# Top-32 selection on rows folded to 304 elements, and both heads transposed in blocks

## The chip, the cores and the metric

The kernel runs on one core of a Trainium2 chip. The metric is the time of one execution in device microseconds, smaller is better; three runs of the kernel before gave 1761.35, 1762.11 and 1762.44, so a median of 1762.11 us. The engines have short names: PE multiplies matrices, PEld is its weight load, DVE is the vector engine, ACT the scalar engine, POOL the general engine, SP issues most transfers. Each works through its own queue in order.

## The reference

Attention in which each query keeps only its 32 highest scores, then a mixer block. The batch is 8, with 8 heads, 576 positions and a head size of 64.

```python
scores = scale * np.matmul(q, k.transpose(0, 1, 3, 2))
kth = np.partition(scores, -top_k, axis=-1)[..., -top_k:-top_k + 1]
mask = scores >= kth
scores = np.where(mask, scores, -1000000000.0)
scores = scores - np.max(scores, axis=-1, keepdims=True)
attn = np.exp(scores)
attn = attn / (np.sum(attn, axis=-1, keepdims=True) + 1e-09)
x = np.matmul(attn, v)          # then (B, H, S, D) -> (B, S, H*D)
h = x.transpose(0, 2, 1) @ U @ V        # rank 32
u = x + h.transpose(0, 2, 1)
out = u + np.maximum(u @ w_ch1, 0.0) @ w_ch2   # 512 -> 2048 -> 512
```

## The kernel before, in words

The 64 heads are taken in 32 pairs (g). A pair is worked off in five steps (t): in steps 0 to 3 a step has 128 queries of both heads, so two score matrices of 128x576; in step 4 the last 64 queries of both heads lie above each other as one matrix of 128x576. There are 160 steps, and n counts them. Five steps are called a period here.

The order of the work is written out by hand: the loop at L702 calls generators, and each engine gets its instructions in just that order. Four parts of different steps overlap in one turn n of the loop:

- `front(n)` finds the 32 highest scores of a row on DVE. MAX8 gives the eight highest (L385, then L400), MATCH_REPLACE8 (L396) overwrites them with a very small number, and so on four times; the last eight hold the threshold. The two heads of a step alternate. The tile `rr` holds the copy of the scores that is worn down.
- The masking of step n-1 follows. For head 0, ACT computes a scaled Relu of threshold minus score (L421) and POOL subtracts it from the scores (L422). For head 1, POOL compares (L403) and adds (L404). Then ACT takes the exponential with its sum (L351, `weigh`) into the tile `E`.
- `scores(n+1)` multiplies q by k on PE (L333, L320 in step 4) and ACT copies the result from PSUM into the tile `Ssb` (L344 to L346, L327).
- The weights must be turned round for the product with v. For head 0 this is done by PE with four transposes (L475) and a copy by ACT (L476), as is the tail of both heads (L480, L481), in `turns`. From step 30 on, outside of step 4 (`shared`), head 1 is turned by `blocks` instead: DVE transposes 32x32 blocks (L447) into the tile `y`, four transfers on SP write it to DRAM in another order (`away`, L453), a fifth brings it back into the tile `PT` (L457). `blocks(n-1)` stands in turn n, after the third round of the search.
- `values(n-2)` multiplies PT by v (L509, L513) on PE. In the queue of PE it stands before `scores(n+1)`.

Between these, `fill` puts the matmuls of the mixer of an earlier batch into PE's queue (L582 with the copy L594, and L601), some at each call, so that they are spread over the steps. When the last step is through, the mixer of the last batch is left and runs alone. In the first 30 steps, `next_params` converts the weights of the mixer from 64 to 32 bits: ACT (L174 to L178), DVE (L186) and POOL (L187, L189) share that. From pair 5 on, q and k are transposed by DVE too (L290), once a period, in step 1.

Of the kernel before, what the change touches and what calls it, by code (L numbers as in the profile page):

```python
# [14 lines left out]
TOPK = 32  # L15
# [11 lines left out]
def kernel(  # L27
# [207 lines left out]
    probs, PTs = {}, {}  # L235
# [74 lines left out]
    def scores(g, t):  # L310
# [4 lines left out]
        S2 = attn.tile([P, 2 * (S + TAIL)], F32, tag="Ssb", name="Ssb", bufs=3)  # L315
        if t == NT:
# [11 lines left out]
            S2s[g, t] = [S2[:, 0:S]]  # L328
# [18 lines left out]
        S2s[g, t] = [S2[:, 0:S], S2[:, S : 2 * S]]  # L347
# [5 lines left out]
    def ways(g, t):  # L353

        if (g, t) == (NPAIR - 1, NT - 1):
            return (0,), (), (1,)
        if (g, t) == (NPAIR - 1, NT):
            return (0,), (), ()  # L360
        return (), (1,) if t < NT else (), (0,)

    def eased(g, t):
        return bool(ways(g, t)[2])

    def front(g, t):
# [6 lines left out]
        chunks, den = S2s.pop((g, t)), dens[g]  # L373
        n = len(chunks)
        E2 = attn.tile([P, 2 * S], F32, tag="E", name="E", bufs=3)
        Es = [E2[:, c * S : (c + 1) * S] for c in range(n)]
        sums = [den[:, 2 * t + c : 2 * t + c + 1] for c in range(n)]
        probs[g, t] = E2
        curs, ms = list(chunks), [None] * n
        first = small.tile([P, 2, 8], F32, tag="first", name="first", bufs=3)  # L380
        nmax = small.tile([P, 2], F32, tag="nmax", name="nmax", bufs=4)
        order = (1, 0) if n == 2 else (0,)
        for c in order:
            ms[c] = first[:, c]
            nc.vector.max(ms[c], curs[c])  # L385
        yield
        early, pooled, gaps = ways(g, t)
        for i in range(1, TOPK // 8):
            if i == 1:
                nc.scalar.mul(nmax[:, 0:n], first[:, 0:n, 0], -SCALE)  # L390
                for c in early:
                    weigh(chunks[c], Es[c], nmax[:, c : c + 1])
            for c in order:

                nxt = attn.tile([P, S], F32, tag="rr", name="rr", bufs=3) if i == 1 else curs[c]
                nc.vector.match_replace(nxt, ms[c], curs[c], NEG)  # L396
                curs[c] = nxt
            for c in order:
                ms[c] = small.tile([P, 8], F32, tag="m8", name="m8", bufs=8)
                nc.vector.max(ms[c], curs[c])  # L400
            yield
        for c in pooled:
            nc.gpsimd.tensor_scalar(Es[c], chunks[c], ms[c][:, 7:8], NEG, ALU.is_lt, ALU.mult)  # L403
            nc.gpsimd.tensor_tensor(chunks[c], chunks[c], Es[c], ALU.add)  # L404
        for c in early:
            nc.vector.scalar_tensor_tensor(
                out=Es[c],
# [10 lines left out]
        for c in gaps:  # L418
            least = small.tile([P, 1], F32, tag="least", name="least", bufs=3)
            nc.scalar.mul(least, ms[c][:, 7:8], WIDEN)  # L420
            nc.scalar.activation(Es[c], chunks[c], AF.Relu, bias=least, scale=-WIDEN)  # L421
            nc.gpsimd.tensor_tensor(chunks[c], chunks[c], Es[c], ALU.subtract)  # L422
            yield
        ahead = pooled if shared(g, t) else ()
        for c in ahead:
            weigh(chunks[c], Es[c], nmax[:, c : c + 1], sums[c])
            yield
        for c in order:
            if c not in early and c not in ahead:
                weigh(chunks[c], Es[c], nmax[:, c : c + 1], sums[c])  # L430
# [9 lines left out]
    def blocks(g, t):  # L440
# [5 lines left out]
        y = attn.tile([P, 4, NT, BLK], F32, tag="y", name="y", bufs=1)  # L446
        nc.vector.transpose(  # L447
            y.rearrange("p r c j -> p c r j"),
            E2[:, S + TAIL : 2 * S].rearrange("p (c r j) -> p c r j", c=NT, r=4),
        )  # L450
        away = dram.tile([P, 4, P], F32, tag="away", name="away")
        for a in range(4):
            nc.sync.dma_start(  # L453
                away[:, a].rearrange("(r i) n -> i r n", r=4),
                y[a * BLK : (a + 1) * BLK].rearrange("i r c j -> i r (c j)"),
            )
        nc.sync.dma_start(  # L457
            PT[:, NT : 2 * NT].rearrange("p a n -> p (a n)"), away.rearrange("p a n -> p (a n)")
        )

    def turns(g, t):
# [9 lines left out]
        for h in range(1 if shared(g, t) else nh):  # L471
# [18 lines left out]
    def values(g, t):  # L490
# [19 lines left out]
        PB = PT[:, NT : 2 * NT].rearrange("p a (c j) -> p c a j", c=NT) if shared(g, t) else None  # L510
        for j in range(NT):
            for h in range(2):
# [3 lines left out]
                    rhs=PB[:, j] if h and shared(g, t) else PT[:, NT * h + j],  # L516
# [325 lines left out]
```

## Time and profile before

| what | value |
|---|---|
| median of three runs | 1762.11 us |
| span of the profiled execution | 1759.8 us |
| PE busy | 1667.1 us, 95% |
| DVE busy | 1535.9 us, 87% |
| ACT busy | 1027.7 us, 58% |
| POOL busy | 847.7 us, 48% |
| L385, L400: MAX8 of 576 elements | 1152, 744 and 748 ns each |
| L396: MATCH_REPLACE8 of 576 elements | 864, 741 and 742 ns each |
| L403, L404, L422: POOL on 576 elements | 2213, 1411, 1418 ns each |
| L447: block transpose of 512 elements | 104, 698 ns each |

The span goes from the first to the last instruction; the rest of an execution's time lies around it, and the runs' median is 2.3 us above this span. "Busy" counts instructions of an engine, not whether something waits for them: PE's instructions are pipelined and their ends are modelled. The duration of a DVE or ACT instruction includes a part in which the next one already runs, so in a timeline the distance of two starts tells what an instruction costs in a row of others. The number in square brackets is how long an engine was idle ahead of an instruction, and on whom it waited.

### The profile page before, as it was taken

Reading aid. Unit: us, or ns where it says so; the run is one execution under the profiler, and the core shown is the slowest. Engines: PE = TensorE matmul, PEld = TensorE weight load, DVE = VectorE, ACT = ScalarE, POOL = GpSimd, SP = SyncE. Lnnn points to the kernel's source line nnn. Section 1 sums busy time; section 2 is a strip of 40 time slices with the busy share of each in tenths; the row PEclk is TensorE's granted clock in tenths of the full one; section 3 lists DMA queues with packets and bytes.
Section 4 is the critical chain, followed back from the end, with each engine's and each line's share of the span. In section 5 each row is a group of like instructions: output and inputs, shape, how many; then the busy total and the mean of one; then the engine's idle time right before and its main releaser. Section 6 shows DMA issues by size and latency. Waiting matters only on the chain.

```text
span 1759.8 us, 28970 instructions
## 1 busy us (share of the span) xinstructions
PE 1667.1 (95%) x9851; PEld 1256.8 (71%) x9851; DVE 1535.9 (87%) x3106; ACT 1027.7 (58%) x2682; POOL 847.7 (48%) x591
## 2 busy tenths in 40 slices
PE   4666889999999999999999999999999999999999
PEld 2444556777777877788777877788777877788677
DVE  7999988999999999999999999999999999994000
ACT  4888777565656556565655665565656656564100
POOL 4788677545454444544445454545454554543000
PEclk7787899999999999999999999999999999999999
DMA  3232231223232222322322222333222232311010
GB/s 91 85 93 84 75 97 41 52 63 76 64 77 65 61 73 59 72 66 67 72 66 66 64 71 64 69 67 73 67 63 71 58 76 58 77 44 46 4 16 13
DMA packets 275828, 112.78 MB, mean 64 GB/s; under 512 B 173920, under 2 KB 260192, under 8 KB 275680
## 3 DMA queue, kind: packets, MB, share of 16 engines
q1 hardware_dynamic: 274624, 110.68, 25.9%
q8 instruction: 77, 1.26, 0.3%
q14 instruction: 71, 0.58, 0.1%
q10 hardware_dynamic: 1056, 0.26, 0.1%
HBM read 74.15 MB, written 36.70 MB: 63 GB/s over the span
## 4 chain that ended last, share of the span: by engine, by line
PE 77%; DVE 16%; POOL 3%; ACT 2%; issue 2%; DMA 1%; SPq 0%; POOLq 0%; DVEq 0%
PE mm L582 26%; PE mm L601 25%; DVE rr L396 7%; PE sc L333 7%; PE O L513 6%; DVE m L400 6%; PE tp L475 3%; DVE first L385 2%; PE sc L320 2%; PE O L499 2%; PE up L557 1%; PE O L509 1%; PE tp L649 1%; PE up L559 1%; PE tp L480 1%
## 5 line engine op out<-in xcount | busy, mean ns | idle before, releaser
L400 DVE MAX8 m<-rr 128x8 f32<-128x576 f32 x864 | 614.4, 748 | 5.5
L601 PE MATMUL mm<-hT,w 128*128 128x256 f32 (+1 forms) x2048 | 547.3, 410 | 0.0
L582 PE MATMUL mm<-uT,w 128*128 128x256 f32 (+1 forms) x2048 | 540.6, 410 | 0.9 <-ACT hT L594 0.9
L403 POOL TENSOR_SCALAR E<-Ssb,m 128x576 f32<-128x576 f32 x127 | 281.1, 2213 | 362.9 <-DVE m L400 345.2
L582 PEld LDWEIGHTS mm<-uT,w 128*128 128x128 f32 x2048 | 371.1, 190 | 115.1 <-issue 26.4
L601 PEld LDWEIGHTS mm<-hT,w 128*128 128x128 f32 x2048 | 368.2, 190 | 107.0 <-issue 22.5
L396 DVE MATCH_REPLACE8 rr<-m,rr 128x576 f32<-128x576 f32 x576 | 423.3, 741 | 0.0
L422 POOL TENSOR_TENSOR Ssb<-Ssb,E 128x576 f32<-128x576 f32 x159 | 225.5, 1418 | 138.1 <-ACT E L421 138.1
L594 ACT ACTIVATE hT<-mm 128x320 f32<-128x320 f32 (+1 forms) x256 | 105.2, 411 | 242.9 <-PE mm L582 242.4
L351 ACT ACTIVATE E<-Ssb,nmax 128x576 f32<-128x576 f32 x288 | 223.0, 775 | 38.1 <-POOL Ssb L404 27.1
L385 DVE MAX8 first<-Ssb 128x8 f32<-128x576 f32 x288 | 203.7, 744 | 37.3 <-ACT Ssb L346 36.6
L396 DVE MATCH_REPLACE8 rr<-first,Ssb 128x576 f32<-128x576 f32 x288 | 211.8, 742 | 0.0
L404 POOL TENSOR_TENSOR Ssb<-Ssb,E 128x576 f32<-128x576 f32 x127 | 179.2, 1411 | 10.6
L333 PE MATMUL sc<-qkT 64*128 64x288 f32 x1024 | 171.2, 456 | 8.8 <-ACT Ssb L344 7.8
L475 PE MATMUL tp<-ident,E 128*128 128x128 f32 x736 | 117.0, 285 | 40.5 <-ACT E L351 16.8
L513 PE MATMUL O<-PT,va 128*64 128x128 f32 x2048 | 146.3, 286 | 1.5 <-DMA PT<-away 1.5
L475 PEld LDWEIGHTS tp<-ident,E 128*128 128x128 f32 x736 | 92.4, 146 | 72.4 <-ACT E L351 20.1
L476 ACT COPY PT<-tp 128x512 f32<-128x512 f32 x184 | 107.0, 586 | 59.3 <-PE tp L475 57.9
L513 PEld LDWEIGHTS O<-PT,va 128*64 128x64 f32 x2048 | 114.5, 141 | 18.2 <-issue 1.8
L333 PEld LDWEIGHTS sc<-qkT 64*128 64x128 f32 x1024 | 93.5, 198 | 47.2 <-issue 15.2
L421 ACT ACTIVATE E<-Ssb,least 128x576 f32<-128x576 f32 x159 | 123.3, 776 | 5.2
L614 DVE TENSOR_TENSOR oT<-uT,mm 128x320 f32<-128x320 f32 (+1 forms) x8 | 3.6, 454 | 137.4 <-PE mm L601 137.4
(81 smaller groups left out, 1565.4 us busy)
## 6 DMA issues: line engine op xcount, KB each, us to landing
away<-y SPq DMA_DIRECT2D x416, 64.0 KB, 1.8
PT<-away SPq DMA_DIRECT2D x104, 256.0 KB, 2.6
raw<-in_moe_w_ch_dram SPq DMA_DIRECT2D x32, 512.0 KB, 3.8
va<-in_v_dram SPq DMA_DIRECT2D x64, 128.0 KB, 2.2
out_dram<-ob SPq DMA_DIRECT2D x57, 128.0 KB, 2.0
ld<-in_q_dram SPq DMA_DIRECT2D x108, 64.0 KB, 2.4
ld<-in_k_dram SPq DMA_DIRECT2D x108, 64.0 KB, 2.3
ld<-in_q_dram SPq DMA_DIRECT2D x108, 8.0 KB, 2.0
```

Source lines behind the costliest of these rows:

```text
L333: nc.tensor.matmul(sc[:, h, 0:HALF], lhsT=qkT[half(h), 0, cols(t)], rhs=qkT[half(h), 1, i * HALF : (i + 1) * HALF], start=True, stop=True,)
L351: nc.scalar.activation(E, chunk, AF.Exp, bias=nmax, scale=SCALE, accum_out=total)
L385: nc.vector.max(ms[c], curs[c])
L396: nc.vector.match_replace(nxt, ms[c], curs[c], NEG)
L400: nc.vector.max(ms[c], curs[c])
L403: nc.gpsimd.tensor_scalar(Es[c], chunks[c], ms[c][:, 7:8], NEG, ALU.is_lt, ALU.mult)
L404: nc.gpsimd.tensor_tensor(chunks[c], chunks[c], Es[c], ALU.add)
L422: nc.gpsimd.tensor_tensor(chunks[c], chunks[c], Es[c], ALU.subtract)
L475: nc.tensor.transpose(tp[:, j, :], E2[:, a : a + P], ident)
L513: nc.tensor.matmul(O[half(h)], lhsT=va[:, h, j, :], rhs=PB[:, j] if h and shared(g, t) else PT[:, NT * h + j], start=False, stop=(j == NT ...
L582: nc.tensor.matmul(ph[:, 0:w], lhsT=w1[:, cc, f * P : (f + 1) * P], rhs=uT[:, cc, lo:hi], start=(cc == 0), stop=(cc == NC - 1),)
L601: nc.tensor.matmul(po[:, 0:w], lhsT=w2[:, f, c * P : (c + 1) * P], rhs=hTs[f][:, 0:w], start=(f == 0), stop=(f == NF - 1),)
```

## The change

A row of 576 scores is folded before it is searched. `upper` takes the larger of element i and element i+288, and `lower` the smaller. Of the 32 highest, at most 16 can lie in `lower`, since for each of these its partner in `upper` is at least as high. So two rounds of MAX8 on the 288 elements of `lower` find its 16 highest, they are written behind the 288 of `upper`, and the four rounds run on these 304 elements. `lower` is computed by POOL on the bits taken as integers: the sum of both halves (`fold`, right after the scores of step n+1), less the maximum that DVE computes (`split`, before the last round of the search of step n). The first step of all is not folded.

The masking of both heads of a shared step is now by Relu on ACT and subtraction on POOL; before step 30, head 1 takes the form in which DVE multiplies the exponential by the mask (L406 before, L446 after). The exponential is written over the scores, `Ssb` has four buffers and not three, and `rr` is gone.

`blocks` transposes both heads, its transfers are twice as large, and `turns` has no more transposes of main parts in shared steps, only those of the tail.

```diff
-        S2 = attn.tile([P, 2 * (S + TAIL)], F32, tag="Ssb", name="Ssb", bufs=3)
+        S2 = attn.tile([P, 2 * (S + TAIL)], F32, tag="Ssb", name="Ssb", bufs=4)
...
+    def fold(g, t):
+        if 0 < g + t and g < NP:
+            upper = attn.tile([P, 2, HALF + TOPK // 2], F32, tag="upper", name="upper")
+            lower = attn.tile([P, 2, HALF], F32, tag="lower", name="lower", bufs=1)
+            folds[g, t] = upper, lower
+            pair(g, t, 0)
+
+    def split(g, t):
+        if (g, t) in folds:
+            pair(g, t, 1)
+
+    def pair(g, t, stage):
+        S2 = S2s[g, t]
+        n = S2.shape[1]
+        upper, lower = folds[g, t]
+        top, bottom = upper[:, 0:n, 0:HALF], lower[:, 0:n].bitcast(U32)
+        a, b = S2[:, :, 0:HALF], S2[:, :, HALF:S]
+        if stage == 0:
+            nc.gpsimd.tensor_tensor(bottom, a.bitcast(U32), b.bitcast(U32), ALU.add)
+        else:
+            nc.vector.tensor_tensor(top, a, b, ALU.max)
+            nc.gpsimd.tensor_tensor(bottom, bottom, top.bitcast(U32), ALU.subtract)
...
-        return (), (1,) if t < NT else (), (0,)
+        if t == NT:
+            return (), (0,)
+        return ((), (1, 0)) if shared(g, t) else ((1,), (0,))
...
+        if folded:
+            upper, lower = folds.pop((g, t))
+            curs = [upper[:, c] for c in range(n)]
+            spots = [[upper[:, c, HALF + i : HALF + i + 8] for c in range(n)] for i in (0, 8)]
+            for c in order:
+                nc.vector.max(spots[0][c], lower[:, c])
+            for c in order:
+                nc.vector.match_replace(lower[:, c], spots[0][c], lower[:, c], NEG)
+            for c in order:
+                nc.vector.max(spots[1][c], lower[:, c])
...
-        for c in pooled:
-            nc.gpsimd.tensor_scalar(Es[c], chunks[c], ms[c][:, 7:8], NEG, ALU.is_lt, ALU.mult)
-            nc.gpsimd.tensor_tensor(chunks[c], chunks[c], Es[c], ALU.add)
...
-        for c in gaps:
-            least = small.tile([P, 1], F32, tag="least", name="least", bufs=3)
-            nc.scalar.mul(least, ms[c][:, 7:8], WIDEN)
-            nc.scalar.activation(Es[c], chunks[c], AF.Relu, bias=least, scale=-WIDEN)
-            nc.gpsimd.tensor_tensor(chunks[c], chunks[c], Es[c], ALU.subtract)
+        if gaps:
+            lo, hi = min(gaps), max(gaps) + 1
+            least = small.tile([P, 2], F32, tag="least", name="least", bufs=3)
+            nc.scalar.mul(least[:, lo:hi], m8[:, lo:hi, 7], WIDEN)
+            for c in gaps:
+                gap = attn.tile([P, S], F32, tag="E", name="E")
+                nc.scalar.activation(
+                    gap, chunks[c], AF.Relu, bias=least[:, c : c + 1], scale=-WIDEN
+                )
+                nc.gpsimd.tensor_tensor(chunks[c], chunks[c], gap, ALU.subtract)
             yield
...
-        y = attn.tile([P, 4, NT, BLK], F32, tag="y", name="y", bufs=1)
-        nc.vector.transpose(
-            y.rearrange("p r c j -> p c r j"),
-            E2[:, S + TAIL : 2 * S].rearrange("p (c r j) -> p c r j", c=NT, r=4),
-        )
-        away = dram.tile([P, 4, P], F32, tag="away", name="away")
+        y = attn.tile([P, 4, 2, NT, BLK], F32, tag="y", name="y", bufs=1)
+        for h in (1, 0):
+            a = h * (S + TAIL)
+            nc.vector.transpose(
+                y[:, :, h].rearrange("p r c j -> p c r j"),
+                E2[:, a : a + MAIN].rearrange("p (c r j) -> p c r j", c=NT, r=4),
+            )
+        away = dram.tile([P, 4, 2 * P], F32, tag="away", name="away")
...
-            PT[:, NT : 2 * NT].rearrange("p a n -> p (a n)"), away.rearrange("p a n -> p (a n)")
+            PT[:, 0 : 2 * NT].rearrange("p a n -> p (a n)"), away.rearrange("p a n -> p (a n)")
...
-        for h in range(1 if shared(g, t) else nh):
+        for h in range(0 if shared(g, t) else nh):
...
@@ the loop, turns of the steps that are shared
         if n + 1 < STEPS:
             scores(*divmod(n + 1, CH))
+            fold(*divmod(n + 1, CH))
         next(here, None)
...
         if away:
             blocks(*divmod(n - 1, CH))
         fill()
         if n <= STEPS:
             turning = turns(*divmod(n - 1, CH))
         fill()
+        split(*divmod(n + 1, CH))
         next(here, None)
```

`fold` and `split` are put into the loop's earlier branches in the same places: after the scores, and before the last round of the search.

## Prediction

> **What bounds the kernel now.** I read the span in stretches of time first, because a share over the whole span mixes stages.
>
> ```profile
> 50.00:100.00 50.00, 33.94 (x216) 22.55 (x214) 49.59 (x104) 40.64 (x97) 39.69 (x28) 0.79 0.30 87
> 457.00:1557.00 1100.00, 1099.42 (x6668) 835.96 (x6667) 1052.12 (x2113) 656.63 (x1756) 527.56 (x352) 1.00 0.29 67
> 1607.00:1760.00 153.00, 147.74 (x655) 116.80 (x653) 7.23 (x16) 21.02 (x53) 3.31 (x5) 1.00 0.07 14
> ```
>
> The columns are the stretch, its length, and busy time of PE, PEld, DVE, ACT and POOL. Up to 200 us DVE has no gap (49.59 of 50). From about 310 to 1607 us PE has none (1099.4 of 1100), but DVE is close behind (1052, 96%). The last 153 us are the last batch's mixer on PE, which the change does not touch. So there are three stages, and I price each by itself: A, the first 20 steps (DVE); B, 200 to 307 us; C, 26 periods of five steps. A period in C lasts 50.05 us.
>
> Next the timeline of DVE in C, for the price of one instruction, and the chain of PE.
>
> ```profile
> 836.42 1.42 DVE L385 MAX8 first<-Ssb 128x8 f32<-128x576 f32 x2 [0.41 <-ACT Ssb L346]
> 843.31 0.70 DVE L447 STREAM_TRANSPOSE y<-E 128x512 f32<-128x512 f32 x1
> 855.31 1.42 DVE L385 MAX8 first<-Ssb 128x8 f32<-128x576 f32 x2 [1.02 <-ACT Ssb L346]
> 862.20 0.07 DVE L396 MATCH_VALUE_LOAD rr<-m,rr 128x8 f32 x1
> 863.64 1.41 DVE L400 MAX8 m<-rr 128x8 f32<-128x576 f32 x2
> 864.97 1.40 DVE L385 MAX8 first<-Ssb 128x8 f32<-128x576 f32 x2
> ```
> ```profile
> 852.28 1.02 PE O L513 x16
> 853.30 1.17 PE sc L333 x8
> 857.36 0.44 PE tp L475 x4
> ```
>
> Starts, not durations, give the price, since neighbours overlap: two maxima take 864.97-863.64 = 1.33, so 0.665 each; two loads with replacements 863.64-862.20 = 1.44, so 0.72 each. A whole step of two heads is 864.97-855.31 = 9.66. The block transpose is 0.61 when followed by other work.
>
> Last, SP's queue, the transfers, and ACT's copies of the scores.
>
> ```profile
> 844.03 1.76 SPq L453 DMA_DIRECT2D away<-y  x4
> 847.18 0.34 SPq L457 DMA_DIRECT2D PT<-away  x1
> ```
> ```profile
> away<-y SPq DMA_DIRECT2D x416, 64.0 KB, 1.8
> PT<-away SPq DMA_DIRECT2D x104, 256.0 KB, 2.6
> raw<-in_moe_w_ch_dram SPq DMA_DIRECT2D x32, 512.0 KB, 3.8
> va<-in_v_dram SPq DMA_DIRECT2D x64, 128.0 KB, 2.2
> ```
> ```profile
> 854.03 0.64 ACT L344 COPY Ssb<-sc 128x576 f32<-128x576 f32 x1 [0.42 <-PE sc L333]
> ```
>
> The blocks leave SBUF at 844.03 and their way back is issued at 847.18; with 2.6 they are there at 849.78. Their reader, the value matmuls at L513, starts at 852.28: the round trip has 2.5 us to spare. The scores of the step after next stand behind these matmuls in PE's queue.
>
> **The change, part by part.** *PE loses* four transposes a pair step: 0.44 x 4 = 1.76 per period, and PE alone would run at 48.3. Over 26 periods that is 46 us, the most that C can gain.
>
> *DVE.* At the slope that the transposes of 512 and 1152 elements show (0.61 and 1.29 from start to start, so 1.06 ns an element) 576 elements take 0.61, which leaves 0.05 for each instruction. So 288 elements cost 0.36, 304 cost 0.38, and a value load adds 0.06. A pair step's search is then 2 x (0.36 + 0.42 + 0.36 + 0.38) + 3 x 2 x (0.44 + 0.38) = 7.97, and the new maximum over 2x288 is 0.66: 8.63 against 9.66. If instead each short instruction cost its 0.14 of latency too, it would be about 10.3; but the pairs alternate, as now, and I take 8.63. The second block transpose gives 0.61 back. The single-head step is about even: its dependent instructions now start 0.8 apart (0.5 at the new length, but there are ten of them), 5.35 and the maximum against 5.7. DVE's work per period is 4 x (7.97 + 1.22) + 5.3 + 3.0 (maxima) + 1.4 = 46.5, no longer a bound.
>
> *ACT* gains a Relu (0.68) and loses a copy of 512 (0.65): nothing, it is 60% busy. *POOL* goes from 5.1 to 5.6 us per pair step (four of 1.41), still half idle.
>
> *SP* issues the same five transfers, each with twice the bytes. The two transposes end 7.66 after the step's first instruction (6.35 of search, 0.61 + 0.70) where one ended at 7.59; that is even. The return trip: 128 KB takes 2.2 and 256 KB 2.6, so 512 KB is 3.4 by that slope, between 2.6 (no growth) and 3.8 (the 512 KB row). The way out, 1.8 now, takes 2.0, between 1.8 and 2.2. Growth together 1.0, from 0 to 1.6.
>
> *The new wait.* Today the search of the next step starts 0.03 after ACT's copies. Now POOL adds the halves, DVE takes the maximum, POOL subtracts, and the search's first instruction (L412, over the lower half) waits for the subtraction; all of DVE stands behind it. Copies to search: 0.07 + 1.41 + 0.09 + 1.41 + 0.05 = 3.0. And DVE's maximum reads two tensors while POOL works. What such a meeting does is in stage A:
>
> ```profile
> 191.51 0.80 DVE L406 SCALAR_TENSOR_TENSOR E<-Ssb,m,E 128x576 f32<-128x576 f32 x1
> ```
> ```profile
> 191.67 1.81 POOL L187 TENSOR_TENSOR w<-w,raw 128x512 uint32<-128x512 uint32 x1 [3.54 <-DVE w L186]
> ```
> ```profile
> 235.03 1.40 POOL L422 TENSOR_TENSOR Ssb<-Ssb,E 128x576 f32<-128x576 f32 x1
> ```
> ```profile
> 235.10 1.61 DVE L186 TENSOR_SCALAR w<-w 128x512 uint32<-128x512 uint32 x1
> ```
>
> L187, 1.29 alone, took 1.81 behind a DVE instruction with two inputs: 0.52 of waiting, just till that ended. And L186, 0.40 alone, took 1.61 behind POOL. So where maximum and addition become ready together, one follows the other: plus 0.6, together 3.6. I take 3.6, with 3.0 as its lower end.
>
> **The sum for C.** The round trip now closes on itself: blocks of step n-1 leave in step n, feed the value matmuls in step n+1, behind these the scores of step n+2. From the first instruction of one step to that of the step after next, today's need is 7.6 (transposes) + 3.15 + 2.6 (landing) + 1.1 (L513) + 2.0 (853.30 to the end of the copies and DVE) = 16.5; the trace has 855.31-836.42 = 18.9, the same 2.4 to spare. With 1.0 for the bytes and 3.6 for the new wait it is 21.1, and the ends are 19.5 and 21.7.
>
> Steps of a period, t = 0 to 4. From t=0 to t=1 no blocks pass: 8.65. From t=1 to t=3 DVE's own work is 9.9 + 1.29 (L290) + 9.9 = 21.05; its maximum is ready at 7.6 while POOL's addition runs till about 7.8 to 8.2 (last maximum, bias, two Relus, two subtractions 3.9, exponential 4.8, copies 6.3, addition 7.8), so 21.4. From t=3 to the next t=0 DVE has but 7.2 in the single step, so the round trip decides: 21.1. Together 51.15, against 50.05 now: +1.1 a period, x 26 = +29 us. The ends are 49.2 (21.05 + 19.5 + 8.65: -22 us) and 52.4 (+61 us). PE's gain of 46 us goes into waits at L513 and at the scores.
>
> **A and B.** Stage A has four periods of 46.75. There the second head keeps its exponential ahead and DVE multiplies by the mask (0.69), so DVE's pair step is 8.63 + 0.69 = 9.32 against 9.66: -1.4 a period if nothing waits. But POOL holds parameter additions (L187, L189, 2.6 a pair, up to two pairs a step) besides its three of 1.41, up to 9.5 of some 10 us, ahead of and between addition and subtraction. The maximum can wait up to one of these, 1.4 a pair step. So -1.4 to +4.2 a period; I take the middle, +1.4, x 4 = +6 (from -6 to +17). In B DVE is only 90% busy; two periods, nothing, 2 us either way.
>
> The profiled execution's span is 1759.8; +35 makes 1794.8. The runs' median is 2.3 above that span, so 1797.
>
> The Trainium skill, SBUF — State Buffer, section Who interferes with whom, says that a Vector instruction with two SBUF inputs and a GpSimd instruction that reads SBUF shut each other out for the whole instruction. The rows above show one direction for two inputs; by the rule the maximum itself also waits for every POOL instruction that it meets, stage A would stand near +17 and the estimate by it would be 1808.
>
> **Rivals.** *The round trip stays hidden, and it is faster.* For it: 2.4 us to spare today, and PE waited for PT only twice (3.3 us in total). Against it: the new wait alone, 3.0, is more than that. It decides at the sum of byte growth and wait: with about 3.6 the period is 50.05 (21.4 + 16.5 + 3.6 + 8.65); I have 4.6. With no growth and no meeting of the two engines it gives 49.2 a period and -6 in A: 1734; if the bound were PE alone, 48.3, it would be 1762 - 46 - 6 = 1710.
>
> *Stores hold the blocks.* SP's queue is in order, and an output store waits there for ACT's copy (L651). Before, blocks transposed by 833.26 left only at 837.25, 4.0 us late, at no cost thanks to the slack. Two outputs fall into a period; if one of them costs 1 to 2 us, C is 26 to 52 us worse: 1823 to 1849.
>
> *It cancels:* the engines do not exclude each other, bytes as taken: 21.05 + 20.5 + 8.65 = 50.2, +4 in C and -6 in A: about 1760.
>
> **How the numbers follow.** Forecast 0.52 (its own range 1775 to 1820), stores 0.19, hidden round trip 0.23, cancelling 0.06. A measurement tells about 0.2%, 3.5 us. The range reaches to 1736, which keeps the nearer part of the faster rival, and to 1848; outside are about 0.15. Faster 0.25 (the hidden round trip and a part of the cancelling), same 0.04, slower 0.71.
>
> **What would show it.** Right: PE in C at about 94% and waiting at L513 for PT or at the scores; idle DVE before L412 by POOL; the DVE search with starts 0.36 to 0.38 apart; PT back in about 3.4 us; a step's period near 51. Wrong: PE still without gaps in C with a period under 49.5 means that the return trip did not decide; maxima of 2x288 that never stretch beside POOL take the 0.6 out; starts above 0.45 apart would make DVE the bound; a longer stage A than +17 would mean that I misjudged POOL's queue.

## The result and the profile after

The changed kernel takes 1930.47 us (median of four runs, 1929.11 to 1933.11) where the kernel before takes 1762.28: a ratio of 1.0956, with an interval of 1.0941 to 1.0972. It is slower, as forecast, but by 168 us and not by 35, and 1930 lies far outside the forecast range. The span of the profiled execution is 1927.7 us, 167.9 more than before.

To see where these 167.9 us arose I took the start of each step from DVE's timeline (the first instruction of its search, L385 before and L412 after) and compared the two kernels stretch by stretch.

| stretch | before, us | after, us | difference | forecast |
|---|---|---|---|---|
| start to step 20 (stage A) | 198.9 | 221.0 | +22.1 | +6 |
| steps 20 to 30 (stage B) | 108.5 | 124.0 | +15.5 | 0 |
| steps 30 to 155 (25 periods of stage C) | 1248.2 | 1376.1 | +127.9 | +28 |
| from step 155 on | 204.2 | 206.6 | +2.4 | +1 |

So three quarters of the loss lie in stage C, where a period went from 49.93 to 55.04 us (51.15 was forecast). The stretches of time of the kernel after, with the columns as before (stretch, length, busy time of PE, PEld, DVE, ACT, POOL, then granted clock, DMA share, GB/s):

```profile
50.00:100.00 50.00, 29.12 (x178) 19.34 (x176) 46.56 (x137) 37.59 (x86) 37.79 (x27) 0.73 0.24 71
345.00:1721.00 1376.00, 1249.41 (x7169) 922.67 (x7168) 1186.65 (x3525) 754.54 (x2000) 735.91 (x550) 0.97 0.38 98
```

In C no engine is full any more: PE is at 91% (1249.41 of 1376), DVE at 86%. In stage A DVE, which had no gap before, now has 3.4 us of them in 50. Where all engines have gaps, waits set the time. Those between 450 and 1700 us (who waited for whom: total us, times, longest) are:

```profile
DVE upper L372 <- ACT Ssb L348: 86.2, 40, 4.9
DVE upper L412 <- POOL lower L373: 70.3, 48, 1.8
PE O L560 <- DMA PT<-away: 70.2, 43, 3.2
PE up L604 <- ACT Tb L600: 17.0, 18, 1.7
```

DVE waits for the copies of the scores (L348), then once more for POOL's subtraction (L373). PE waits for PT to come back from DRAM, and now and then for something the forecast never named: `Tb`, the low-rank product of the mixer.

DVE's timeline of one period shows the prices of the change (start, duration, then in brackets the idle time ahead and on whom it waited):

```profile
901.34 1.92 DVE L372 TENSOR_TENSOR upper<-Ssb 128x576 f32<-128x576 f32 x1
...
904.85 0.82 DVE L412 MAX8 upper<-lower 128x8 f32<-128x288 f32 x2
905.58 0.07 DVE L414 MATCH_VALUE_LOAD lower<-upper,lower 128x8 f32 x1
...
926.27 0.76 DVE L372 TENSOR_TENSOR upper<-Ssb 128x576 f32<-128x576 f32 x1 [1.34 <-ACT Ssb L348]
...
929.82 0.82 DVE L412 MAX8 upper<-lower 128x8 f32<-128x288 f32 x2 [1.14 <-POOL lower L373]
...
949.17 0.76 DVE L372 TENSOR_TENSOR upper<-Ssb 128x576 f32<-128x576 f32 x1 [1.25 <-ACT Ssb L348]
...
952.73 0.82 DVE L412 MAX8 upper<-lower 128x8 f32<-128x288 f32 x2 [1.84 <-POOL lower L373]
```
```profile
901.24 1.40 POOL L370 TENSOR_TENSOR lower<-Ssb 128x576 uint32<-128x576 uint32 x1 [2.57 <-issue]
...
949.27 1.93 POOL L370 TENSOR_TENSOR lower<-Ssb 128x576 uint32<-128x576 uint32 x1 [3.00 <-issue]
951.28 1.42 POOL L373 TENSOR_TENSOR lower<-lower,upper 128x576 uint32<-128x576 uint32 x1
```

Three things are to be seen. From the start of two maxima over 288 elements to the next instruction it is 905.58 - 904.85 = 0.73, so 0.365 each: the search is as cheap as forecast. Where DVE's maximum and POOL's addition met, the second to start (L370 at 949.27, where DVE had waited for the scores, or L372 at 901.34) took 1.9 instead of 1.4 or 0.76. And the search then waits for the subtraction: from the start of L372 to that of L412 it is 952.73 - 949.17 = 3.56, the forecast new wait.

The transfers of the page (KB each, median us from issue to landing):

```profile
away<-y SPq DMA_DIRECT2D x416, 128.0 KB, 2.4
PT<-away SPq DMA_DIRECT2D x104, 512.0 KB, 3.3
```

### The profile page after: what moved, and what is told of

It reads as the page before. It is cut to its first block, busy times and chain, and to the rows that moved or that the text cites. A ratio compares the mean times of both kernels' runs of the same rounds, so it can differ in the third digit from the quotient of the medians.

```text
span 1927.7 us, 29923 instructions
## 1 busy us (share of the span) xinstructions
PE 1679.0 (87%) x9435; PEld 1235.3 (64%) x9435; DVE 1542.5 (80%) x4559; ACT 1037.0 (54%) x2659; POOL 994.8 (52%) x759
## 3 DMA queue, kind: packets, MB, share of 16 engines
q8 instruction: 74, 1.21, 0.3%
## 4 chain that ended last, share of the span: by engine, by line
DVE 26%; PE 23%; issue 8%; DMA 7%; ACT 4%; POOL 4%; SPq 2%; DVEq 0%; POOLq 0%; ACTq 0%
PE mm L629 9%; DVE upper L438 7%; PE mm L648 7%; DVE m L443 6%; DMA PT<-away 5%; DVE upper L372 3%; POOL lower L373 2%; PE O L560 2%; DVE y L494 2%; DVE lower L414 2%; DVE upper L412 2%; DVE first L426 2%; DVE upper L416 2%; PE sc L335 2%; ACT E L464 2%
## 5 line engine op out<-in xcount | busy, mean ns | idle before, releaser
L370 POOL TENSOR_TENSOR lower<-Ssb 128x576 uint32<-128x576 uint32 (+1 forms) x159 | 235.6, 1482 | 535.6 <-ACT nmax L431 225.7
L443 DVE MAX8 m<-upper 128x8 f32<-128x304 f32 x858 | 366.5, 463 | 3.3
L438 DVE MATCH_REPLACE8 upper<-m,upper 128x304 f32<-128x304 f32 x572 | 258.0, 457 | 0.0
L373 POOL TENSOR_TENSOR lower<-lower,upper 128x576 uint32<-128x576 uint32 (+1 forms) x159 | 204.8, 1288 | 73.3 <-DVE upper L372 67.8
L377 ACT ACTIVATE Ssb<-Ssb,nmax 128x576 f32<-128x576 f32 x263 | 203.9, 775 | 71.0 <-POOL Ssb L467 70.0
L372 DVE TENSOR_TENSOR upper<-Ssb 128x576 f32<-128x576 f32 (+1 forms) x159 | 148.8, 936 | 111.2 <-ACT Ssb L348 105.0
L560 PE MATMUL O<-PT,va 128*64 128x128 f32 x2048 | 152.2, 295 | 84.4 <-DMA PT<-away 84.3
L412 DVE MAX8 upper<-lower 128x8 f32<-128x288 f32 x286 | 117.1, 445 | 100.1 <-POOL lower L373 100.1
L560 PEld LDWEIGHTS O<-PT,va 128*64 128x64 f32 x2048 | 119.2, 146 | 104.6 <-DMA PT<-away 94.7
L494 DVE STREAM_TRANSPOSE y<-Ssb 128x512 f32<-128x512 f32 x208 | 137.4, 687 | 5.2 <-ACT Ssb L377 1.7
L438 DVE MATCH_REPLACE8 upper<-first,upper 128x304 f32<-128x304 f32 x286 | 129.1, 457 | 0.0
L414 DVE MATCH_REPLACE8 lower<-upper,lower 128x288 f32<-128x288 f32 x286 | 124.5, 441 | 0.0
```

The source lines that it names most:

```text
L370: nc.gpsimd.tensor_tensor(bottom, a.bitcast(U32), b.bitcast(U32), ALU.add)
L372: nc.vector.tensor_tensor(top, a, b, ALU.max)
L373: nc.gpsimd.tensor_tensor(bottom, bottom, top.bitcast(U32), ALU.subtract)
L377: nc.scalar.activation(E, chunk, AF.Exp, bias=nmax, scale=SCALE, accum_out=total)
L560: nc.tensor.matmul(O[half(h)], lhsT=va[:, h, j, :], rhs=PB[:, h, j] if shared(g, t) else PT[:, NT * h + j], start=False, stop=(j == NT - 1),)
```

## Two chains in stage C

Before the experiments I split the five steps of a period. A length is the distance of two starts, the mean over the steps from 30 on; experiments stand in the same table.

| kernel | t=0 | t=1 | t=2 | t=3 | t=4 | period |
|---|---|---|---|---|---|---|
| before | 9.66 | 11.54 | 10.40 | 10.26 | 8.07 | 49.93 |
| after | 9.22 | 11.75 | 11.78 | 9.82 | 12.47 | 55.04 |
| e1, one head in blocks | 9.05 | 11.65 | 11.94 | 9.11 | 10.72 | 52.47 |
| e2, search of before, both heads in blocks | 9.73 | 12.14 | 10.98 | 10.97 | 8.60 | 52.43 |
| e3, scores first | 9.22 | 11.46 | 11.02 | 9.54 | 9.60 | 50.86 |
| e4, lower half by DVE | 9.82 | 12.61 | 11.62 | 10.11 | 10.86 | 55.06 |
| e5, low-rank work later | 9.42 | 11.66 | 10.82 | 10.52 | 11.99 | 54.39 |
| e6, e3 and e5 | 9.10 | 11.27 | 10.02 | 9.81 | 10.58 | 50.82 |
| e9, before with scores first | 9.65 | 11.54 | 10.59 | 10.53 | 8.23 | 50.54 |

For the stretch from the start of t=3 to the next t=0 I followed the members of the round trip one by one, each the mean of 25 periods:

| member | forecast | measured |
|---|---|---|
| start of the step to the end of the two block transposes | 7.66 | 7.63 |
| wait in SP's queue | 0 | 0.07 |
| first way out to the issue of the way back | 3.35 | 3.79 |
| issue of the way back to the value matmuls | 3.4 | 3.41 |
| value matmuls (with what stands between them and the scores) | 1.1 | 1.30 |
| scores and copies | 2.0 | 2.54 |
| copies to the search (addition, maximum, subtraction) | 3.6 | 3.58 |
| sum | 21.1 | 22.3 |

So the loop that was forecast is there, and it is 1.2 us longer, in the way out (transfers of 128 KB land after 2.4, where 2.0 was taken) and in the scores. In the chain of waits its last links look like this:

```profile
1040.56 3.58 DMA PT<-away
...
1044.19 1.09 PE O L560 x16
1045.28 1.12 PE sc L323 x8
```

The stretch from t=1 to t=3 takes 11.75 + 11.78 = 23.5, where 21.4 was forecast from DVE's own work. PT is not late there: from the issue of its way back to the value matmuls it is 5.26 us, 1.9 more than the transfer needs. What stands ahead of the value matmuls in PE's queue is the low-rank part of the mixer (`mixed`; pT at L592, up at L604), once a period, and it waits for copies that ACT makes after the two Relus of the masks, which themselves wait for the last maximum of step t=1. ACT's and PE's timelines:

```profile
1028.04 0.20 ACT L461 ACTIVATE least<-m 128x2 f32<-128x2 f32 x1 [1.92 <-DVE m L443]
1028.28 1.44 ACT L464 ACTIVATE E<-Ssb,least 128x576 f32<-128x576 f32 x2
1029.63 0.24 ACT L528 COPY PT<-tp 128x128 f32<-128x128 f32 x1
1029.77 0.26 ACT L600 COPY Tb<-pT 128x128 f32<-128x128 f32 x1
```
```profile
1030.09 0.81 PE L604 MATMUL up<-V,Tb 128*128 128x320 f32 x2 [0.43 <-ACT Tb L600]
...
1033.76 1.09 PE L560 MATMUL O<-PT,va 128*64 128x128 f32 x16
1034.78 1.24 PE L335 MATMUL sc<-qkT 64*128 64x288 f32 x8
```

From the last maximum (1028.0) it is 2.1 us to `up`, 4.7 more through the low-rank matmuls, the fillers between them and the values to the scores, then copies and fold; the search of t=3 starts at 1040.41. This is a second chain, through ACT's queue, the mixer and PE's queue, and it needs no DMA.

That leaves hypotheses to be told apart. T1: both chains decide C because the scores of the next step stand in PE's queue behind work that waits. R1: DVE's own work, stretched by POOL, decides. R2: it is the larger transfers alone. And for A and B: the masks, or the fold behind POOL's queue.

## Experiments on stage C

**e1: the fold stays, one head is turned by PE as before.** This undoes the second half of the change alone.

```diff
-        for h in (1, 0):
+        for h in (1,):
...
-        away = dram.tile([P, 4, 2 * P], F32, tag="away", name="away")
+        away = dram.tile([P, 4, P], F32, tag="away", name="away")
...
-        for h in range(0 if shared(g, t) else nh):
+        for h in range(1 if shared(g, t) else nh):
```

> The folded search stays, but only head 1 goes through the blocks and the round trip over DRAM; head 0 is transposed by PE again, as before the change. Theory (the round trip blocks, transfers, value matmuls, scores, fold, search closes on itself): the way out falls from 2.4 to 1.8 us, the way back from 3.3 to 2.6, one transpose of 0.6 us goes, so 1.9 us less on each of the two places of a period where the loop decides. A period of stage C falls from 55 to about 51 to 52 us, where PE (50) is close; the time is about 1840 us (1825 to 1865). Rival (POOL's additions in front of the search and the meetings of DVE and POOL are the loss by themselves): nothing that they consist of is touched, the time stays above 1900 us.

Measured: 1860.35 us, a ratio of 1.0554 (1.0523 to 1.0585). The stretch from t=3 to t=0 falls from 22.3 to 19.8; from t=1 to t=3 nothing changes (23.6). Waits between 450 and 1600 us:

```profile
DVE upper L372 <- ACT Ssb L348: 80.1, 48, 2.9
DVE upper L412 <- POOL lower L373: 69.0, 49, 1.8
...
PE O L560 <- DMA PT<-away: 6.6, 14, 0.9
```

With the smaller transfers PE hardly waits for PT (6.6 us against 70.2), and yet the kernel is 98 us slower than before, 37 of them from the time up to step 30 (344.8 against 307.4). R2 falls as the only cause: the transfers decide one of the two stretches, the other one is as long without them.

**e2: the search of before, both heads in blocks.** The other half of the change alone. Only so that it fits, the tile of the blocks lies in the three buffers of the weight loads, where the changed kernel has one buffer of its own.

```diff
-        y = attn.tile([P, 4, NT, BLK], F32, tag="y", name="y", bufs=1)
...
+        y = mlpp.tile([P, 2 * C], U32, tag="raw", name="raw", bufs=3).bitcast(F32)
+        y = y.rearrange("p (r h c j) -> p r h c j", r=4, h=2, c=NT)
+        for h in (1, 0):
...
+        away = dram.tile([P, 4, 2 * P], F32, tag="away", name="away")
...
-        for h in range(1 if shared(g, t) else nh):
+        for h in range(0 if shared(g, t) else nh):
```

> The kernel before (search over 576 elements, masks as before) with both heads in blocks and the larger transfers; the tile of the blocks lies in the buffers of the weight loads so that it fits. Theory: the loop grows by 1.9 us out of the 2.4 us that it had to spare, so it does not close, and PE gets its 1.76 us a period: 49 to 50 us a period, 1725 to 1762 us. Rival (the larger transfers alone make the values late): a period of 52 us or more, above 1800 us.

Measured: 1823.83 us, 1.0347 (1.0269 to 1.0425); a miss, and by its number (a period of 52.43) the rival's. The stretch of time and a wait:

```profile
450.00:1600.00 1150.00, 1084.10 (x6301) 811.99 (x6300) 1105.14 (x2197) 610.79 (x1667) 526.17 (x351) 0.98 0.41 104
```
```profile
PE O L516 <- DMA PT<-away: 63.6, 41, 3.5
```

DVE is at 96%, as in the kernel before, but with one more block transpose in each of four steps (0.61 each, 2.4 a period) there is more to do, and the steps are 0.1 to 0.7 longer. DVE's busy time goes from 47.8 us a period before to 50.4, as much as the period grows, while its waits for the copies of the scores are 1.0 us a period in both: so it is DVE's work that makes the period longer here, and not late values as the rival has it. PE, relieved of its transposes, has gaps and waits for PT. The relief of PE is worth nothing where DVE is nearly full, and the cheaper search is worth nothing where the loop decides; neither half is a gain alone.

**e3: scores(n+1) and the fold ahead of values(n-2).** Only the order in PE's queue changes; all work, transfers and the fold stay. If T1 holds, the round trip is cut, since the scores no longer stand behind PT. The low-rank part keeps its place ahead of the scores.

```diff
-        if n - 2 >= ALONE:
-            values(*divmod(n - 2, CH))
         if n + 1 < STEPS:
             scores(*divmod(n + 1, CH))
             fold(*divmod(n + 1, CH))
+        if n - 2 >= ALONE:
+            values(*divmod(n - 2, CH))
```

> The changed kernel, only that in PE's queue the scores of the step after next stand ahead of the value matmuls that wait for the round trip. Theory: the scores no longer wait for the transfers, the loop is open, and a period of stage C falls from 55 to 50 to 51 us: 1930 less 100 to 130, so 1800 to 1830 us. Rival (POOL's additions and the meetings of DVE and POOL): the copies come a little earlier, but the additions are as long; above 1890 us.

Measured: 1819.12 us, 1.0320 (1.0289 to 1.0352), as T1 said. The period falls from 55.04 to 50.86, 109 us over 26 periods, with not one instruction less: 3.2 us from t=3 to t=0, and 1.1 from t=1 to t=3.

```profile
450.00:1600.00 1150.00, 1115.40 (x6484) 813.94 (x6483) 1072.02 (x3194) 677.75 (x1807) 656.25 (x499) 1.00 0.42 107
```
```profile
999.83 0.76 DVE L372 TENSOR_TENSOR upper<-Ssb 128x576 f32<-128x576 f32 x1 [0.41 <-ACT Ssb L348]
1003.37 0.82 DVE L412 MAX8 upper<-lower 128x8 f32<-128x288 f32 x2 [1.82 <-POOL lower L373]
```

PE is back at 97% and the waits for the copies are short (0.41 here, 1.25 at the same place of the period above; over the whole execution DVE's idle time ahead of L372 falls from 111.2 to 23.2 us); POOL's 1.82 is left in the single-head step. R1, by which the time would have stayed above 1890, falls as the main cause. This is the run that carries the explanation of C, but it cuts one of the two chains and not both. PE's timeline in a step t=2 (it starts at 973.69) has the low-rank part ahead of the scores still:

```profile
975.12 0.70 PE L604 MATMUL up<-V,Tb 128*128 128x320 f32 x2
...
978.46 1.24 PE L335 MATMUL sc<-qkT 64*128 64x288 f32 x8
...
980.05 1.09 PE L560 MATMUL O<-PT,va 128*64 128x128 f32 x16
```

**e9: the same reordering in the kernel before.** Were the order simply better, this would be faster too.

> The kernel before with only the order in PE's queue turned round: scores ahead of the value matmuls. Theory (there the round trip has 2.4 us to spare and PE is the bound): no change, 1755 to 1768 us. Rival (this order is better in any case, and its gain in the changed kernel says nothing on the loop): 1740 us or less.

Measured: 1778.50 us, 1.0086 (1.0065 to 1.0106). It is slightly slower, above the 1755 to 1768 that I had expected; what refutes the rival holds all the more. So the order by itself is worth nothing, and what e3 gained it gained from the waits that the change had made. The wait of the block transposes for the exponential grew, in the stretch from 450 to 1600 us from 19.7 us to

```profile
DVE y L447 <- ACT E L351: 52.8, 39, 2.3
```

**e4: the lower half by DVE, right after the maximum.** This takes POOL's two legs of 1.41 out of the way to the search and gives DVE one more instruction a step.

```diff
-        if stage == 0:
-            nc.gpsimd.tensor_tensor(bottom, a.bitcast(U32), b.bitcast(U32), ALU.add)
-        else:
+        if stage == 1:
             nc.vector.tensor_tensor(top, a, b, ALU.max)
-            nc.gpsimd.tensor_tensor(bottom, bottom, top.bitcast(U32), ALU.subtract)
+            nc.vector.tensor_tensor(lower[:, 0:n], a, b, ALU.min)
```

> The changed kernel, but DVE computes the lower half itself, by a second instruction (minimum of both halves) right behind the maximum; POOL's addition and subtraction are gone. From the copies to the search it is then 2 x 0.66 and a little, about 1.5 us, in place of 3.6. Theory: 2.1 us less at each of the two places of a period where the loop decides, DVE 3 us more work elsewhere: stage C from 55 to about 51.5 us, stages A and B lose the 30 us that they had gained by POOL's queue; about 1810 us (1790 to 1840). Rival (the transfers are the loss, the fold's wait is hidden behind them): stage C stays near 54 to 55 us and only stages A and B gain; about 1890 to 1910 us.

Measured: 1909.97 us, 1.0836 (1.0804 to 1.0867); a miss, the rival's number. C is as long as before this edit (55.06). The round trip from t=3 to t=0 does get shorter, 20.98 against 22.3, and copies to search 2.34 against 3.58. But a minimum in each step is about 3 us of DVE's work a period, t=0 to t=2 are 0.6, 0.9 and -0.2 longer, and PE and DVE wait as before:

```profile
DVE upper L370 <- ACT Ssb L348: 82.5, 49, 4.3
PE O L558 <- DMA PT<-away: 61.7, 38, 3.2
```

So what was gained on one member of the loop was paid for with work on an engine that the other steps need. What e4 gained, it gained in A and B (below).

**e5 and e6: the low-rank part four fillers later,** in the changed kernel (e5) and together with scores first (e6). If the second chain runs through that part, t=2 must become shorter.

```diff
-            mixing.append(mixed((n - 2) // CH, 5))
+            mixing.append(mixed((n - 2) // CH, 9))
```

> The changed kernel with the low-rank matmuls of a head pair (pT and up, once a period) four filler calls later, so that in the turn of step 2 they stand behind the scores and not ahead of the value matmuls. Theory: steps 1 and 2 of a period are late not by the round trip but by this work, which was harmless while the search needed the scores 3.6 us later; both together fall from 23.5 to 21.5 to 22 us, a period from 55 to about 53, and the time to 1880 us (1870 to 1895). Rival (the round trip decides here too, as the prediction had it): steps 1 and 2 stay, above 1915 us.

Measured for e5: 1916.36 us, 1.0871 (1.0849 to 1.0892). The time is the rival's (above 1915), the stretch from t=1 to t=3, at 22.5, lies between the two expectations. t=2 falls by 0.96, but t=3 rises by 0.70. The low-rank wait is gone from the head of the list, and PT takes its place in t=2 (1.64 us a period there, none before this edit):

```profile
PE O L560 <- DMA PT<-away: 77.5, 56, 2.7
```

So the two chains lie close together: with one shortened, the other decides, and the stretch from t=1 to t=3 is only 1.1 us shorter.

> Both moves in PE's queue together: the scores ahead of the value matmuls, and the low-rank work behind both. Theory (two separate causes in one queue): a period of 49.5 to 50 us, DVE 46.5 and the meetings, so 1785 to 1800 us. Rival (one cause, the round trip): as with the scores first alone, 1819 us.

Measured for e6: 1820.56 us, 1.0327 (1.0306 to 1.0348), no gain over e3 and the rival's number. By stretches it looks different: from t=1 to t=3 it is now 21.3, after 22.5 in e3 and in e5 and 23.5 without either, and 21.3 is what the forecast took there for DVE's own work (21.4). So each of the two moves takes away half of that stretch's loss, and in e3 the low-rank part still held it up. But t=4 grows by 1.0: DVE is idle there for 3.2 us in place of 2.3, 0.8 of it ahead of the block transposes, for exponentials. Why these came later was not followed up. PE is at 97% in e3 and in e6, and work that is moved out of one step has to be done in another, but no run shows that this is the reason.

## Experiments on stages A and B

Before the fold, step 30 began at 307.4; now it begins at 345.0. One place in A, in the timelines of POOL and DVE:

```profile
142.09 1.15 POOL L586 TENSOR_TENSOR x<-x,den 128x512 f32<-128x512 f32 x1 [2.34 <-ACT x L585]
143.66 1.29 POOL L187 TENSOR_TENSOR w<-w,raw 128x512 uint32<-128x512 uint32 x1 [0.42 <-ACT raw L178]
145.02 1.69 POOL L189 TENSOR_TENSOR w<-w,raw 128x512 uint32<-128x512 uint32 x1
146.68 1.40 POOL L373 TENSOR_TENSOR lower<-lower,upper 128x576 uint32<-128x576 uint32 x1
```
```profile
141.61 0.73 DVE L372 TENSOR_TENSOR upper<-Ssb 128x576 f32<-128x576 f32 x1
143.92 1.64 DVE L446 SCALAR_TENSOR_TENSOR Ssb<-Ssb,m,E 128x576 f32<-128x576 f32 x1
...
148.11 0.82 DVE L412 MAX8 upper<-lower 128x8 f32<-128x288 f32 x2 [2.54 <-POOL lower L373]
```

The maximum was done at 142.3, but the subtraction started at 146.68: POOL's queue is in order, and it held a normalisation that waited for ACT and the two parameter additions ahead of it. The search waited 2.54 us. DVE's mask multiplication (L446) met POOL as well and took 1.64 instead of 0.8. Which of the two costs the time, the fold or the new masks? Over the first 30 steps DVE's busy time grew by 17.5 us and its idle time by 20.1. Nearly all of the latter is the search's wait for POOL's subtraction (0 to 345 us):

```profile
DVE upper L412 <- POOL lower L373: 19.8, 10, 4.3
```

**e7: the fold only from step 30 on,** and the first 30 steps mask both heads by Relu and subtraction; C is that of the changed kernel.

```diff
-        if 0 < g + t and g < NP:
+        if g * CH + t >= ROUNDED and g < NP:
...
-        return ((), (1, 0)) if shared(g, t) else ((1,), (0,))
+        return (), (1, 0)
```

> The fold begins only with step 30, and the first 30 steps mask both heads by Relu and subtraction, without the mask on DVE; stage C is that of the changed kernel. Theory (the fold in POOL's full queue is the loss in stages A and B): step 30 starts at 300 to 310 us in place of 345, the rest is the same: 1888 to 1898 us. Rival (the lead is lost anyway, since stage C waits at its own pace from whatever start): the same statement; but if A was slow for another reason, the loads or the masks, step 30 stays at 330 us or later and the time above 1910 us.

Measured: 1891.77 us, 1.0731 (1.0710 to 1.0753). Step 30 begins at 307.8, so all 37 us of A and B are given back, and C stays at 55.15.

**e10: the fold stays everywhere, only the mask by DVE goes** (the second half of the diff above).

> The changed kernel, in whose first 30 steps both heads are masked by Relu and subtraction, as in the later ones; the fold stays there. DVE loses the mask (0.69 us a pair step), POOL gets another 1.41. Theory (the search waits for POOL's queue): step 30 starts at 338 to 350 us as in the changed kernel, the time stays at 1922 to 1935 us. Rival (DVE's mask and its meetings with POOL are the loss of the first 30 steps): step 30 at 325 us or earlier, the time 1910 us or less.

Measured: 1935.76 us, 1.0977 (1.0955 to 1.0999), with step 30 at 346.6. The same wait (0 to 346 us), then the stretch from 50 to 200 us in e7, e10 and e4 (in this order):

```profile
DVE upper L412 <- POOL lower L373: 36.8, 12, 4.5
```

```profile
50.00:200.00 150.00, 100.57 (x641) 68.64 (x639) 149.14 (x313) 130.31 (x306) 92.35 (x69) 0.78 0.30 84
```
```profile
50.00:200.00 150.00, 86.62 (x533) 58.32 (x530) 130.42 (x387) 117.29 (x272) 124.39 (x92) 0.74 0.26 76
```
```profile
50.00:200.00 150.00, 91.55 (x580) 62.46 (x579) 149.17 (x456) 113.77 (x259) 80.95 (x54) 0.78 0.28 80
```

The first 30 steps side by side:

| kernel | step 30, us | DVE busy | DVE idle |
|---|---|---|---|
| before | 307.4 | 286.1 | 21.3 |
| after | 345.0 | 303.6 | 41.4 |
| e7, no fold there | 307.8 | 287.7 | 20.1 |
| e10, fold, no mask on DVE | 346.6 | 284.4 | 62.2 |
| e4, fold without POOL | 326.2 | 307.0 | 19.2 |

e7 shows that without the fold, masking both heads by Relu and subtraction costs nothing. In e10 DVE has 20 us of gaps in 150 and the stage is as long as with the mask on DVE, so the rival, that the mask is the loss by itself, falls. But e10 does not show that the mask is free beside the fold: it takes 19 us off DVE's busy time and gives POOL one more subtraction a step, and the search waits 17 us more for POOL (busy for 124 of 150 us). In e4, where the fold does not pass through POOL, DVE has no gap from 50 to 200 us and step 30 begins at 326.2: half of the 37 us is back; DVE, with an extra minimum in each step, is full. In A and B the fold loses either way, by waits for POOL's queue or by DVE's work; in the changed kernel it is about half of each.

## Experiments that put the remedies together

e8 is e6 with the first 30 steps of e7. e11 is e3 with the first 30 steps of e7, and in t=0 the lower half comes from DVE, because POOL's wait was left in the step before it. e12 adds the later low-rank part to e11. The new piece (POOL's addition is left out in t=0 too):

```diff
+            if t == 0:
+                nc.vector.tensor_tensor(lower[:, 0:n], a, b, ALU.min)
+            else:
+                nc.gpsimd.tensor_tensor(bottom, bottom, top.bitcast(U32), ALU.subtract)
```

> All three repairs: scores first, low-rank work later, fold from step 30 on only. Theory (the three causes add up): 1930 less 130 less 40, about 1752 us (1743 to 1765), so about even with the kernel before or a little faster. Rival (there is still another cause in the fold): above 1775 us.

> Scores first, fold and new masks' fold part from step 30 on only, and for step 0 of each pair DVE computes the lower half itself, since it is in the single-head step before it that the search still waits for POOL (0.4 + 1.8 us a period). Theory: a period falls from 50.9 to 48.6 to 49.3 us, close to PE's 48.3; 1785 less 35 to 50, so 1735 to 1750 us, faster than the kernel before. Rival (something else fills the single-head step): above 1765 us.

> The same with the low-rank work behind the scores. Theory: step 2 of a period is 1 us shorter, the single-head step no longer by POOL; 1730 to 1745 us. Rival: as e11, since the work only moves to the next turn.

| run | us | ratio and interval | step 30 | period in C |
|---|---|---|---|---|
| e8 | 1785.14 | 1.0129 (1.0112 to 1.0146) | 304.9 | 50.71 |
| e11 | 1779.15 | 1.0092 (1.0069 to 1.0115) | 302.8 | 50.70 |
| e12 | 1774.77 | 1.0058 (1.0041 to 1.0074) | 304.3 | 50.64 |

All three missed, and the times are the rivals': I expected C under 50 us a period, and it stayed at 50.6 to 50.7 whatever I took away. In e11 t=4 does fall from 9.60 to 8.46, as meant, and t=0 rises from 9.22 to 10.22: DVE is idle in t=0 for 1.3 us in place of 0.4, 0.9 of it where the search of the step after waits for POOL's subtraction, which was 0.2 in e3. So the wait for POOL moved on by one step. PE in e11 between 450 and 1600 us:

```profile
450.00:1600.00 1150.00, 1120.77 (x6532) 820.64 (x6530) 1086.79 (x3221) 681.09 (x1823) 588.39 (x452) 1.00 0.42 107
```

PE is at 97.5%. With four transposes a step less to do than before, its work would fit into 48.3 us a period by the forecast's count, but its busy time is 49.4 in e11, and 49.3 to 49.4 in e2, e3 and e6 too, against 49.9 before: 0.5 less and not 1.76. This count holds more than work, since the same matmuls as before come to 50.5 in e9; so how little PE could need, and what keeps C at 50.6, stays open. What is settled is that the folded kernel with its scores first, without the fold in the first 30 steps and with DVE's minimum in t=0, comes within 0.6% of the kernel before and not below it: no run here beats the kernel before.

## Why the prediction was wrong in size

**Right: the direction and the mechanism.** "The round trip now closes on itself" decided where it was said to (t=3 to t=0), with PE in waits at L560 for PT and DVE idle ahead of L412 by POOL; PE in C is at 91% (94% forecast). e3 shows that the scores' place in PE's queue, behind the values, costs the greater part of the loss in C (4.2 of 5.1 us a period), by changing that alone; that the order itself is no gain is shown by e9. PE's 48.3 a period, the floor under the forecast's gain, was reached in no run.

**Right: the prices.** Starts 0.36 to 0.38 apart in the search; PT back in 3.3 to 3.4 us; 3.58 from the copies to the search against 3.6; the two block transposes done 7.63 after the start against 7.66.

**Wrong: "From t=1 to t=3 DVE's own work is ... 21.05 ... so 21.4."** It was 23.5, 2.1 us a period, 53 us over 25 periods. I asked for the round trip only in the stretch with the short single step, and there only for the transfer. The step that failed is the one in which nothing but DVE was costed: once a period the low-rank part stands in PE's queue ahead of the values, and it waits for ACT behind the Relus. "*ACT* gains a Relu (0.68) and loses a copy of 512 (0.65): nothing" costed ACT by its busy time and not by what stands in its queue behind these Relus; that the Relus are what delays the copy is read from the timeline and was not tested by itself. Before, the search of t=3 followed the copies by 0.40 us; now 3.58 lie between them, and so the copies are needed that much earlier. e1 shows that the stretch needs no larger transfers to be as long; e5 that moving the low-rank part out of it shortens it by 1.1 us, and that the round trip is then next; e3 that the scores ahead of the values shorten it by 1.1 as well; and e6, with both, is at 21.3. So the 21.4 was right for DVE's own work, and the step that failed is that nothing but this work would decide there.

**Wrong: the members of "21.1."** It was 22.3, 1.2 a period, 30 us. The way out (2.0 taken for 128 KB, the upper end was 2.2; measured 2.4) and the values, scores and copies (3.1 against 3.84) were sized too low. The upper end of the forecast, 21.7, was no bound, since it took the widening from rows of transfers of another form and none for PE's part. (The upper end of the period, 52.4, does not follow from the terms given either: 8.65 + 21.4 + 21.7 is 51.75.)

**Wrong: t=0, "no blocks pass: 8.65."** It was 9.22: the maximum beside POOL's addition is stretched there (L372 took 1.15 on average in t=0, against 0.76 alone), which is 0.39 of the 0.57. 14 us over 25 periods. With such meetings in it, DVE's busy time in C did not fall to the 46.5 us a period of the forecast but only from 47.8 to 47.5.

**Wrong: stages A and B, "+1.4 a period" and "nothing".** They lost 37.6 us, 31.6 more than forecast, and two terms failed by about as much. I priced the wait for POOL by one parameter addition (1.4); in the place shown the subtraction stood behind three foreign instructions and one of their waits, 4.3 us after the maximum was done, and in all the search waited 19.8 us. And DVE's own work, forecast to fall from 9.66 to 9.32 a pair step, grew by 17.5 us in 30 steps: the mask (L446) took 1.04 on average where the same form took 0.79 before (L406), and the maximum over two heads 1.21 where it takes 0.76 alone. I took B for free because DVE was "only 90% busy" there; its periods went from about 54 to 62, 3.9 us by work and 3.8 by waits. An idle share is no cover for a chain in which every member waits for the one before.

Together 53 + 30 + 14 + 32 = 129 of the 133 us between the forecast and the result; the rest is the base of the sum, where I took 50.05 for the period before and its mean is 49.93.

**The rivals.** The hidden round trip and the cancelling case fell with the loop. "Stores hold the blocks" gave a number closer to the result (up to 1849), but by another mechanism: blocks did wait in SP's queue behind a store, 0.45 us on average in t=2 (at most 2.2), but 0.07 in t=3, whose blocks decide.

**The Trainium skill's rule** (SBUF — State Buffer, section Who interferes with whom), that a Vector instruction with two SBUF inputs and a GpSimd instruction that reads SBUF shut each other out: this case's trace agrees, now in both directions. L372 took 1.92 behind L370, and L370 took 1.93 behind L372; over its 127 instructions on two heads L372 took 1.04 on average, so 0.28 x 127 = 35 us more of DVE's time than at 0.76 each. The estimate by the rule, 1808, was nearer than mine, but the larger part of the loss does not hang on that: in e3 these 127 instructions take 1.04 on average too, and the time is 111 us less.

## What to carry to other kernels

When a change puts a wait ahead of an engine that was never idle, list for each turn everything that stands in the in-order queues ahead of the item that is now needed earlier, foreign work and what that work waits for included; each of it becomes part of the loop, and slack that was counted to the old need is gone. Price a closed loop in every stretch of the period and not only in the one with the shortest step: here two chains lay within about 1 us of each other, so that shortening one moved the time by only 14 us, while taking the scores out from behind the other gave 111. And a gain on one engine (PE's transposes, DVE's search) is only worth what the chain of waits leaves of it: each half of this change by itself made the kernel slower.

## What the hardware showed that was not expected

- The exclusion of DVE and POOL takes the later one, whichever it is, and its cost is most of the time until the earlier ends: L370 took 1.93 in place of 1.40 when L372 had started 0.10 earlier (0.53, with 0.66 to go till L372's end), L372 took 1.92 in place of 0.76 when L370 had started 0.10 earlier (1.16, with 1.30 to go).
- Twice the bytes made the transfers through DRAM a quarter to a third longer: the way out went from 1.8 us for 64 KB to 2.4 for 128 KB (2.0 was forecast), the way back from 2.6 for 256 KB to 3.3 for 512 KB (3.4 was forecast).
- The granted clock of PE in C was 0.97 in the changed kernel, where PE is at 91%, and 1.00 in the kernel before and in e3, where it is at 97% or more. I did not measure what that is worth by itself.
